# Decoding with an integer add, and TensorE turns for queries, keys and attention weights of two batches

## The chip, the cores and the metric

One core of a Trainium2 chip runs the whole program. The metric is device microseconds (us) from one launch to its end. A run of the kernel before stands at a median of 836.11 us over 3 runs.

## What is computed

Eight batches, eight heads, 576 tokens, head size 64, 32 memory slots.

```
a = softmax(phi, over the 32 slots)                # b h s m
k_m = einsum('bhsm,bhsd->bhmd', a, k)              # memory keys
v_m = einsum('bhsm,bhsd->bhmd', a, v)              # memory values
scores = (q @ k_m^T) / 8                           # b h s m
attn = softmax(scores, over the 32 slots)
x = (attn @ v_m), heads side by side               # 4608 x 512
h = x @ w_in;  g = relu(h)**2;  out = g @ w_out    # d_ff 2048
```

q, k, v and phi are float32. The two weights, w_in and w_out, are float64 and come to the device as pairs of 32-bit words (a low and a high word per number) and are decoded on the chip into a high and a low float32r part.

## The kernel before

**Planning.** Every operation is recorded by `op`, `vec` or `dma` with a guessed cost for each engine that may do it, with the buffers that it reads and writes, and with a due time. `Plan.order` then schedules them all: on each engine the ready operation with the earliest due time goes first; those marked `lead` are treated as due 9000 ns earlier. The result is one in-order list for each engine: TensorE (PE), VectorE (DVE), ScalarE (ACT), GpSimd (POOL) and SyncE (SP). SP issues nearly all loads, in its order. A buffer name (`tag`) has one or two slots; a new user of a slot waits until the last user is done.

**Work of a batch.** `memory` forms k_m and v_m for four heads (half `hh`), with phi, k and v in `phi` and `KV` tiles: a maximum on DVE (`mx`), two turns on PE (`pmx`), the exponential on ACT, then the sums and products `pkv` on PE (L421, L408). v_m goes into a block-diagonal tile `VT`, k_m into a turned block-diagonal tile `kb`. `attention` calls `scores` for each half: queries are turned in 32x32 blocks by DVE (`qT`, L527), multiplied on PE with `kb` as the stationary operand (`psc`, L532), turned back in 32x32 blocks by DVE into `S` (L536), normalised there (L544 to L551), turned a third time by DVE (`at`, L566) and split into two parts `ath` and `atl` (L260, L570).

**Weights and steps.** `decode` turns one 512 KB load of raw words (`raw`) into a weight tile; there are 16 pieces for w_in (`wi`) and 16 for w_out (`wo`), each a half of `piece`. `vw_alone` multiplies `VT` with a piece of w_in into `vw` (x @ w_in is formed as attn @ (v_m @ w_in)). `step` g does one tile of 128 of d_ff for one batch: `mm1` gives h (L603) and its squares `gh`, `glo`, `gl`; `mm2` adds them times `wo` into `acc` (L633, L634, L636).

**Decode** of one piece, on tiles of 128x512: the high word is clipped on DVE (L322), scaled on ACT (L323), its sign is taken (L324) and joined with the shifted rest (L325), giving the float `W`. Then the power of two of `W` is cut out (L326), the low word is multiplied by 2^-52 and by that power (L327), and the product is added to `W` (L330). ACT copies the sum into the high part; DVE subtracts (L339) to get the low part. For the pieces of w_out other than j = 0 (14 of 32) L330 is left out and the product is added to the low part by an accumulating DMA that POOL issues (L343).

**Order in the program.** Batch 0's memory and attention, then four times a piece of w_in, one of w_out and two steps of batch 0; batch 1's memory and attention and its first eight steps; then the other four pieces of each weight. From batch 2 on everything is decoded. Decoded w_in goes to DRAM too (L346) and is read back for later batches (L351). The tiles in which pieces are decoded (`raw` and `work`) are slots that other data uses later; the last pieces use the slots of `q` and `KV`.

Of the kernel before, what the change touches and what calls it, by code (L numbers as in the profile page):

```python
# [206 lines left out]
def tile_attention_moe(  # L207
# [97 lines left out]
    def decode(kind, j, h, room):  # L305
# [20 lines left out]
        vec({"DVE": ts(ND)}, lambda e: nc.vector.tensor_scalar(T(), W(), POWER, None, ALU.bitwise_and), [wk], [tk], lead=True)  # L326
        vec({"DVE": tt(ND)}, lambda e: nc.vector.scalar_tensor_tensor(tf(), low(), 2.0 ** -52, tf(), ALU.mult, ALU.mult), [rk, tk], [tk], lead=True)  # L327
        late = kind == "wo" and j > 0
        if not late:
            vec({"DVE": tt(ND)}, lambda e: nc.vector.tensor_add(wf(), wf(), tf()), [tk, wk], [wk], lead=True)  # L330
# [43 lines left out]
    def memory(b, hh, where=None):  # L374
# [70 lines left out]
        op({"PE": 300}, lambda e: nc.tensor.transpose(pv()[:, 0:P], vx().rearrange("p r d -> p (r d)"), ident), [vx], [pv], lead=True, lat=300)  # L445
        vh, vl = VT[b]
        for s in (0, 1):
            ch = 2 * hh + ((s + b) % 2)
# [4 lines left out]
            vec({"DVE": tt(64)}, lambda e, src=src, hi=hi, lo=lo: nc.vector.tensor_sub(lo(), src(), hi().bitcast(F32)),
                [pv, (vh, (ch, s))], [(vl, (ch, s))], port=None, lead=True)

# [218 lines left out]
    def evac(a, home, o, cols, add=False):  # L674
# [5 lines left out]
        for j in range(0, 4, n):  # L680
            b, c = cols[j]

            def store(d, j=j, b=b, c=c):
                rows = out[b * S:(b + 1) * S, :].rearrange("(p c) e -> c p e", c=NC)
                d(rows[c:c + n], o()[32 * j:32 * (j + n), :])
# [108 lines left out]
```

## Time and profile before

| | |
|---|---|
| three runs | 831.14, 836.11, 837.33 us |
| span of the profiled execution | 831.4 us, 12939 instructions |
| busy in the span | PE 763.5, DVE 571.2, ACT 378.1, POOL 67.4 us |
| mean granted TensorE clock | 0.973 |
| read from memory, written | 79.17 MB, 17.83 MB |

The page gives the profiled execution's span and no other time for it; the span stands beside the lowest of the three runs, 831.14 us. Rows of the page name a line, an engine, an operation, output<-input, and behind the bar the busy time in us, the mean duration of one in ns, and the idle time of the engine just before it with what ended it. PEld is the loading of stationary operands, which overlaps PE.

### The profile page before, as it was taken

The numbers are of one execution on the slowest core, as the hardware profiler recorded it, in microseconds if no ns is written. First come the engines' busy times: TensorE is split into PE (matmuls) and PEld (weight loads), VectorE is DVE, ScalarE is ACT, GpSimd is POOL, SyncE is SP. The second block draws the span as 40 slices with busy tenths as digits, with TensorE's granted clock in tenths as the row PEclk, the third lists the DMA queues.
The fourth block names the chain that finished last, engine by engine and source line by source line (L and its number), as shares of the span: only waits on it lengthen the run. The fifth ranks groups of instructions, "written<-read, shape, count | busy, mean of one in ns | idle before, by whom it ended". The sixth has DMA issues, their size and how long they took to land.

```text
span 831.4 us, 12939 instructions
## 1 busy us (share of the span) xinstructions
PE 763.5 (92%) x4756; PEld 643.3 (77%) x4756; DVE 571.2 (69%) x1266; ACT 378.1 (45%) x871; POOL 67.4 (8%) x105
## 2 busy tenths in 40 slices
PE   3468789989989899999999999999999999999995
PEld 2245578878768688888888888888788888888884
DVE  3899899898446756696768465786768556774540
ACT  1235466656535245563436355463435355552320
POOL 3113112222100100001000100000000100000000
PEclk9959999999999899999999999999999999999998
DMA  7947966657665443322552533323422433100001
GB/s 210 302 153 223 261 192 203 178 174 212 159 161 151 116 132 102 102 80 52 143 142 72 135 111 99 117 54 81 140 61 69 138 93 99 53 16 36 1 1 63
DMA packets 93091, 101.56 MB, mean 122 GB/s; under 512 B 24868, under 2 KB 78116, under 8 KB 93028
## 3 DMA queue, kind: packets, MB, share of 16 engines
q1 hardware_dynamic: 80292, 81.55, 33.2%
q0 software_dynamic: 12736, 19.19, 9.5%
q8 instruction: 37, 0.61, 0.3%
q14 instruction: 26, 0.21, 0.1%
HBM read 79.17 MB, written 17.83 MB: 117 GB/s over the span
## 4 chain that ended last, share of the span: by engine, by line
PE 73%; issue 10%; DVE 8%; DMA 3%; ACT 2%; POOL 2%; SPq 0%; POOLq 0%; DVEq 0%; ACTq 0%
PE h L603 20%; PE acc L636 12%; PE acc L633 12%; PE acc L634 12%; PE accl L659 4%; PE pvw L494 4%; PE psc L532 3%; PE pkv L408 3%; DMA q<-in_q_dram 2%; PE pvw L475 1%; DVE vw L503 1%; DVE qT L527 1%; ACT vw L260 1%; DMA wo<-work 1%; DVE work L325 1%
## 5 line engine op out<-in xcount | busy, mean ns | idle before, releaser
L603 PE MATMUL h<-ath,vw 128*128 128x320 f32 (+1 forms) x1024 | 213.9, 300 | 8.9 <-ACT ath L260 6.3
L633 PE MATMUL acc<-wo,gh 128*128 128x512 f32 x512 | 207.0, 404 | 2.7 <-ACT gh L609 2.5
L634 PE MATMUL acc<-wo,gh 128*128 128x512 f32 x512 | 201.7, 394 | 0.0
L603 PEld LDWEIGHTS h<-ath,vw 128*128 128x128 f32 x1024 | 172.5, 190 | 25.7 <-ACT ath L260 6.7
L636 PE MATMUL acc<-wo,glo 128*128 128x512 f32 x512 | 161.5, 409 | 3.0 <-DVE glo L613 2.8
L503 DVE TENSOR_TENSOR vw<-pvw,vw 64x256 fp32r<-64x256 f32 x192 | 78.5, 420 | 68.0 <-ACT vw L260 66.2
L633 PEld LDWEIGHTS acc<-wo,gh 128*128 128x128 f32 x512 | 97.1, 190 | 23.3 <-ACT gh L609 3.8
L260 ACT CAST vw<-pvw 64x256 fp32r<-64x256 f32 (+1 forms) x206 | 74.9, 381 | 83.9 <-PE pvw L494 37.6
L603 PE MATMUL h<-atl,vw 128*128 128x256 f32 (+1 forms) x512 | 110.5, 297 | 0.0
L634 PEld LDWEIGHTS acc<-wo,gh 128*128 128x128 f32 x512 | 96.9, 189 | 16.9
L636 PEld LDWEIGHTS acc<-wo,glo 128*128 128x128 f32 x512 | 90.5, 191 | 21.4 <-DVE glo L613 7.6
L609 ACT ACTIVATE gh<-r 128x512 fp32r<-128x512 f32 x128 | 80.7, 631 | 45.3 <-DVE r L608 38.5
L613 DVE TENSOR_TENSOR glo<-r,gh 128x512 fp32r<-128x512 f32 x128 | 87.6, 684 | 5.1 <-ACT r L611 2.9
L608 DVE TENSOR_SCALAR r<-h 128x256 f32<-128x256 f32 (+1 forms) x109 | 49.7, 458 | 59.0 <-PE h L603 58.1
L607 ACT ACTIVATE r<-h 128x256 f32<-128x256 f32 (+1 forms) x147 | 58.8, 407 | 67.8 <-PE h L603 59.8
L603 PEld LDWEIGHTS h<-atl,vw 128*128 128x128 f32 x512 | 83.0, 190 | 0.5 <-DVE atl L570 0.2
L611 ACT ACTIVATE r<-r 128x576 f32<-128x576 f32 x93 | 63.7, 685 | 2.1
L610 ACT ACTIVATE gl<-r 128x64 fp32r<-128x64 f32 x128 | 32.7, 256 | 63.2 <-DVE r L608 61.0
L659 PE MATMUL accl<-wo,gl 128*128 128x512 f32 x192 | 53.0, 400 | 0.1
L532 PE MATMUL psc<-qT,kb 128*128 128x256 f32 (+1 forms) x128 | 43.3, 465 | 5.8 <-DVE S L536 3.1
L494 PE MATMUL pvw<-wi,VTh 128*128 128x256 f32 x192 | 38.1, 290 | 3.8 <-DVE vw L503 3.7
L659 PEld LDWEIGHTS accl<-wo,gl 128*128 128x128 f32 x192 | 35.4, 191 | 7.3 <-DVE o L260 0.5
(94 smaller groups left out, 818.5 us busy)
## 6 DMA issues: line engine op xcount, KB each, us to landing
wi<-w_in_hi SPq DMA_DIRECT2D x56, 256.0 KB
wi<-w_in_lo SPq DMA_DIRECT2D x56, 256.0 KB
q<-in_q_dram SPq DMA_DIRECT2D x32, 288.0 KB
KV<-in_k_dram SPq DMA_DIRECT2D x32, 256.0 KB
KV<-in_v_dram SPq DMA_DIRECT2D x32, 256.0 KB
raw<-in_moe_w_in_dram SPq DMA_DIRECT2D x16, 512.0 KB
raw<-in_moe_w_out_dram SPq DMA_DIRECT2D x16, 512.0 KB
out_dram<-o POOLq DMA_DIRECT2D x20, 256.0 KB, 8.4
```

Of the source, the lines that this page charges most:

```text
L260: nc.scalar.copy(o, i) if e == "ACT" else ENG[e].tensor_copy(o, i)
L494: nc.tensor.matmul(pw()[:, x * SL:(x + 1) * SL], l()[:, 2 * hh + x, :], w(r, x), start=(i == 0), stop=(i == 2))
L503: vec({"DVE": tt(SL)}, lambda e, V=V, pr=pr, src=src: nc.vector.tensor_sub(V()[pr, 1, hh, :], src(), V()[pr, 0, hh, :].bitcast(F32)), [pw, ...
L532: nc.tensor.matmul(pq()[:, 0:32 * n], kb()[:, x].rearrange("p h m -> p (h m)"), qT()[:, x, 0:n].rearrange("p c t -> p (c t)"), start=(x == ...
L603: nc.tensor.matmul(p()[:, 0:n], V()[:, l, hh, c0:c0 + P], x()[:, hh, cs], start=(i == 0), stop=(i == 5))
L609: op({"ACT": act(SM)}, lambda e: nc.scalar.activation(gh(), r()[:, 0:SM], AF.Square), [r], [gh])
L611: op({"ACT": act(S), **({} if b < 2 else {"DVE": tt(S)})}, lambda e: nc.scalar.activation(r(), r(), AF.Square) if e == "ACT" else nc.vecto ...
L613: vec({"DVE": tt(SM)}, lambda e: nc.vector.tensor_sub(glo(), r()[:, 0:SM], gh().bitcast(F32)), [r, gh], [glo])
L633: nc.tensor.matmul(a(), gh()[:, c], t()[:, 0], start=f0, stop=False)
L634: nc.tensor.matmul(a(), gh()[:, c], t()[:, 1], start=False, stop=False)
L636: nc.tensor.matmul(a(), glo()[:, c], t()[:, 0], start=False, stop=f1)
L659: nc.tensor.matmul(a(), G()[:, l, :], t()[:, w], start=(ff == 0 and n == 0), stop=(ff == NFF - 1 and n == 2))
```

## The change

It has two parts.

*Decode.* The low word is converted by ACT in place, in the raw tile, with a scale of 2^-29, from uint32 to uint32, that is rounded to an integer in units of the last place of `W`. DVE then adds that integer to the bits of `W`. The cut of the power (L326), the product (L327) and the accumulating DMA (L343) go; all 32 pieces are added in the same way.

*Batches 0 and 1.* `memory_turned` and `attention_turned` take the place of the end of `memory` and of `attention`. Products with an identity on PE, which land in PSUM, turn k_m (together with v_m), the queries (`pq`, and `pql` for the 64 tokens left of 576) and the weights (`pat`, `patl`). Scores now have the queries as the stationary operand and `kb` as the moving one, so that they land with tokens on partitions (`psc`, `left`) and the normalising reads them from PSUM. Batch 0 uses the two PSUM slots `h`, batch 1 the one slot `pa`. Queries are loaded as 128x2x256 and 64x2x64 instead of as 64x1152, four DMAs for a half instead of two. Output rows of the two batches are stored in the order that follows from this.

```diff
-        vec(.. tensor_scalar(T(), W(), POWER, None, ALU.bitwise_and), [wk], [tk], lead=True)
-        vec(.. scalar_tensor_tensor(tf(), low(), 2.0 ** -52, tf(), ALU.mult, ALU.mult), [rk, tk], [tk], lead=True)
-        late = kind == "wo" and j > 0
-        if not late:
-            vec(.. tensor_add(wf(), wf(), tf()), [tk, wk], [wk], lead=True)
+        op({"ACT": act(ND)}, .. activation(low(), low(), AF.Copy, scale=2.0 ** -29), [rk], [rk], lead=True)
+        vec({"DVE": tt(ND)}, .. tensor_tensor(W(), W(), low(), ALU.add), [rk, wk], [wk], lead=True)
...
-        if late:
-            dma(.. d(out=part(1), in_=tf(), accum_op=ALU.add), 4096 * P, [tk, k1], [k1], eng="POOL", lead=True)
...
+        if b < 2:
+            memory_turned(b, hh, u, pk, rs, KV[0][0])
+            return
...
+    def memory_turned(b, hh, u, pk, rs, KV):
...
+        kb = kTs[b, hh] = st([P, 4, 2, M], F32, "kb", f"kb{u}", 2)
+        op({"POOL": 250}, lambda e: nc.gpsimd.memset(kb(), 0.0), [], [kb], lead=True)
+        vec({"DVE": 290}, .. tensor_scalar_mul(kd(), two(0), rs()), [pk, rs], [KV], ..)
+        vec({"DVE": 350}, .. vx() = two(1) * rs() * par ..)
+        for i, x, t in ((1, kd, KV), (0, vx, vx)):
+            op({"PE": 150}, .. nc.tensor.transpose(pv()[:, i * P:(i + 1) * P], x().., ident), ..)
+        for x in (0, 1):
+            op({"ACT": act(P), "DVE": tt(P)}, .. copy(e, kb()[pr, :, x, :], pv()[pr, P:2 * P]..), ..)
+        values(b, hh, pv)
...
+    def attention_turned(b):
...
+        bank = lambda name: pt("h", name, 2) if b == 0 else pt("pa", name)
+        late = pt("pv", f"left{b}")
...
+            for x in (0, 1):
+                pq = bank(f"pq{u}_{x}")     # four transposes of Q, 128x128, then a copy to qT
...
+            pq = bank(f"pql{u}")            # four transposes of QL, 64x64, then a copy to rest
...
+            psc = bank(f"psc{u}")
+            def mm(e, psc=psc, qT=qT, kb=kb):
+                for h in range(4):
+                    for y in (0, 1):
+                        nc.tensor.matmul(s4[:, 2 * y:2 * y + 2, h, :], qT()[:, h, y, :], kb()[:, h].., start=True, stop=True)
...
+            softmax(Sm, psc, NMAIN * P, psc, Sm, u)
+            if hh == 1:
+                softmax(Sl, lambda: late()[:, 0:P], P, late, (rest, 2), f"l{b}")
+        for hh in (0, 1):
+            pat = bank(f"pat{b}_{hh}")      # four transposes of Sm, a copy to ath, a difference to atl
...
+        pat = bank(f"patl{b}")              # one transpose of Sl, a copy to ath, a difference to atl
...
-    attention(0)
+    attention_turned(0)
...
-    attention(1)
+    attention_turned(1)
```

The planner gives a new order on every engine. Three places, before and after; lines of after.py differ from those of the kernel before.

The first instructions of PE, before: the turns for the first half of batch 0, then its sums with `ones` and its products with k and v.

```order
L393 MATMUL pmx_0_102<-ident,mx_0_95 128x128
L396 MATMUL pmx_0_102<-ident,mc_0_106 128x128
L421 MATMUL pkv_0_116<-ones,phi_0_78 32x1 x20
L408 MATMUL pkv_0_116<-KV_0_0_84,phi_0_78 32x128 x2
L408 MATMUL pkv_0_116<-KV_0_1_97,phi_0_78 32x128 x2
```

The same place in the changed kernel; `pq` are the turned queries, `q` their load.

```order
L386 MATMUL pmx_0_104<-ident,mx_0_95 128x128
L389 MATMUL pmx_0_104<-ident,mc_0_110 128x128
L521 MATMUL pq_0_0_171<-ident,q_0_117 128x128 x4
L521 MATMUL pq_0_1_183<-ident,q_0_117 128x128
L414 MATMUL pkv_0_121<-ones,phi_0_78 32x1 x20
L401 MATMUL pkv_0_121<-KV_0_0_84,phi_0_78 32x128 x2
```

Five turns of queries now stand ahead of the sums of the first half.

SP's loads behind the first KV tiles, before: phi of the second half, its k and v, the queries of the first half, the first raw words.

```order
L359 DMA phi_1_91<-in_phi_dram 128x4x128
L360 DMA phi_1_91<-in_phi_dram 64x4x32
L359 DMA KV_1_0_113<-in_k_dram 128x2x256
L360 DMA KV_1_0_113<-in_k_dram 64x2x64
L359 DMA KV_1_0_113<-in_v_dram 128x2x256
L360 DMA KV_1_0_113<-in_v_dram 64x2x64
L359 DMA KV_1_1_141<-in_k_dram 128x2x256
L360 DMA KV_1_1_141<-in_k_dram 64x2x64
L359 DMA KV_1_1_141<-in_v_dram 128x2x256
L360 DMA KV_1_1_141<-in_v_dram 64x2x64
L515 DMA q_0_166<-in_q_dram 64x1152 x2
L320 DMA raw<-in_moe_w_in_dram 128x2x512 x2
```

The same place in the changed kernel (behind these come the other two loads of k and v for `KV_1_1`, the queries of the second half, `q_1`, and only then the first raw words).

```order
L352 DMA phi_1_91<-in_phi_dram 128x4x128
L353 DMA phi_1_91<-in_phi_dram 64x4x32
L509 DMA q_0_117<-in_q_dram 128x2x256
L510 DMA ql_0_119<-in_q_dram 64x2x64
L509 DMA q_0_117<-in_q_dram 128x2x256
L510 DMA ql_0_119<-in_q_dram 64x2x64
L352 DMA KV_1_0_146<-in_k_dram 128x2x256
L353 DMA KV_1_0_146<-in_k_dram 64x2x64
L352 DMA KV_1_0_146<-in_v_dram 128x2x256
L353 DMA KV_1_0_146<-in_v_dram 64x2x64
L352 DMA KV_1_1_176<-in_k_dram 128x2x256
```

The queries of the first half moved ahead of k and v of the second half, and those of the second half moved ahead of the first raw words.

DVE behind the exponential of the first half, before: the first blocks of queries, then decode.

```order
L527 STREAM_TRANSPOSE qT_0_0_205<-q_0_166 128x2x256
L322 TENSOR_SCALAR work<-raw 128x512
L324 TENSOR_SCALAR work<-raw 128x512
L433 TENSOR_SCALAR rs_1_271<-pkv_1_210 128x1
L434 RECIPROCAL rs_1_271<-rs_1_271 128x1
L325 SCALAR_TENSOR_TENSOR work<-work 128x512
L322 TENSOR_SCALAR work<-raw 128x512
L326 TENSOR_SCALAR work<-work 128x512
L324 TENSOR_SCALAR work<-raw 128x512
L327 SCALAR_TENSOR_TENSOR work<-raw,work 128x512
```

The same place in the changed kernel; `S` holds the exponentials of the first half's scores, `rz` their sums.

```order
L496 TENSOR_REDUCE rz_0_271<-S_0_252 128x16
L259 COPY rest_205<-pql_1_266 64x256
L497 TENSOR_SCALAR rz_0_271<-rz_0_271 128x16
L498 RECIPROCAL rz_0_271<-rz_0_271 128x16
L499 TENSOR_TENSOR S_0_252<-S_0_252,rz_0_271 128x512
L321 TENSOR_SCALAR work<-raw 128x512
L323 TENSOR_SCALAR work<-raw 128x512
L426 TENSOR_SCALAR rs_1_364<-pkv_1_284 128x1
L324 SCALAR_TENSOR_TENSOR work<-work 128x512
L321 TENSOR_SCALAR work<-raw 128x512
L326 ISA work<-raw,work 128x1024
```

The end of the normalising of the first half (its maxima and differences stand just ahead of these rows) now comes before the first decode instruction, which used to come before any of it; the integer add is the instruction that reads 128x1024 elements.

More of the change, by code (lines that the diff above doesn't have):

```diff
@@ L340, in decode @@
             [wk, k0], [k1], lead=True)
-        if late:
-            dma(lambda d: d(out=part(1), in_=tf(), accum_op=ALU.add), 4096 * P, [tk, k1], [k1], eng="POOL", lead=True)
         if kind == "wi":
@@ L454, in memory @@
                 [pv, (vh, (ch, s))], [(vl, (ch, s))], port=None, lead=True)
+    def memory_turned(b, hh, u, pk, rs, KV):
+        vx = st([P, 2, D], F32, "vx", f"vx{u}")
+        kd = lambda: KV()[:, 0:2 * D].rearrange("p (r d) -> p r d", r=2)
+        two = lambda i: pk()[:, i * D:(i + 1) * D].rearrange("p (o d) -> p o d", o=1).broadcast_to([P, 2, D])
+        kb = kTs[b, hh] = st([P, 4, 2, M], F32, "kb", f"kb{u}", 2)
+        op({"POOL": 250}, lambda e: nc.gpsimd.memset(kb(), 0.0), [], [kb], lead=True)
+        vec({"DVE": 290}, lambda e: nc.vector.tensor_scalar_mul(kd(), two(0), rs()), [pk, rs], [KV], port=None, lead=True)
+        vec({"DVE": 350}, lambda e: nc.vector.scalar_tensor_tensor(
+            vx(), two(1), rs(), par.rearrange("p (r o) -> p r o", o=1).broadcast_to([P, 2, D]), ALU.mult, ALU.mult), [pk, rs], [vx], port=None, lead=True)
+        pv = pt("pa", f"pvt{u}")
+        for i, x, t in ((1, kd, KV), (0, vx, vx)):
+            op({"PE": 150}, lambda e, i=i, x=x: nc.tensor.transpose(pv()[:, i * P:(i + 1) * P], x().rearrange("p r d -> p (r d)"), ident),
+               [t], [(pv, i)], lead=True, lat=300)
+        for x in (0, 1):
+            pr = slice(64 * x, 64 * x + 64)
+            op({"ACT": act(P), "DVE": tt(P)}, lambda e, x=x, pr=pr: copy(e, kb()[pr, :, x, :], pv()[pr, P:2 * P].rearrange("p (h m) -> p h m", h=4)),
+               [(pv, 1), kb], [(kb, x)], lead=True)
+        values(b, hh, pv)
@@ L683, in store @@
             def store(d, j=j, b=b, c=c):
[L684 to L685 removed]
+                rows = out[b * S:(b + 1) * S, :]
+                if b >= 2:
+                    rows = rows.rearrange("(p c) e -> c p e", c=NC)[c:c + n]
+                elif c < 4 * NMAIN:
+                    rows = rows[0:SM].rearrange("(p c) e -> c p e", c=NMAIN)[c // 4]
+                else:
+                    rows = rows[SM:S]
+                d(rows, o()[32 * j:32 * (j + n), :])
             dma(store, 32 * n * DM * 4, [home], [], eng="SP" if b >= B - 2 else "POOL")
```

76 lines of the change are left out of this document (72 added, 4 removed).

## The prediction

> **What bounds the kernel now.** I read the page's busy times first, then a table by stretches of the span (time, then busy us and count for PE, PEld, DVE, ACT, POOL, then granted clock, DMA share and GB/s), then who PE waits for.
>
> ```profile
> PE 763.5 (92%) x4756; PEld 643.3 (77%) x4756; DVE 571.2 (69%) x1266; ACT 378.1 (45%) x871; POOL 67.4 (8%) x105
> ...
> 0.00:57.40 57.40, 25.99 (x277) 15.90 (x277) 40.29 (x90) 13.61 (x25) 10.98 (x21) 0.84 0.73 218
> 57.40:110.00 52.60, 39.88 (x252) 30.46 (x252) 48.54 (x108) 24.94 (x56) 14.23 (x19) 0.92 0.84 239
> 110.00:170.00 60.00, 55.27 (x324) 48.36 (x325) 54.91 (x120) 38.06 (x84) 10.36 (x13) 1.00 0.63 186
> 170.00:210.00 40.00, 39.97 (x240) 35.63 (x240) 33.88 (x66) 25.43 (x55) 9.52 (x12) 1.00 0.68 194
> 210.00:290.00 80.00, 72.11 (x495) 58.41 (x494) 48.15 (x108) 33.26 (x80) 6.29 (x12) 0.94 0.58 149
> 290.00:360.00 70.00, 69.85 (x396) 61.10 (x395) 45.66 (x103) 36.38 (x94) 1.34 (x2) 0.99 0.39 114
> ```
>
> PE is idle for 831.4 - 763.5 = 67.9 us. Of that 31.4 lie before 57.4 us, when the first steps begin, 12.7 between 57.4 and 110, 4.7 up to 170, 7.9 between 210 and 290, 0.2 up to 360. What is left, 11 us, is nearly all the tail. So from 290 us on the kernel is bound by PE, and the change, which touches nothing there, can only move that part as a whole. Up to 110 us PE waits and DVE is the busy one: 48.5 of 52.6 us in the second stretch. All decode and both changed batches lie before 290 us; **the question is how much of 56.7 us of idle PE goes, and how much PE work comes.**
>
> **Term 1, DVE up to the fourth `vw` of batch 0**, the L483 at 106.7 us in the first row here. Below it stand the groups of DVE up to 107 us that the change removes or shortens (count | busy us, mean ns | idle):
>
> ```profile
> 106.70 0.68 DVE L483 TENSOR_TENSOR vw<-pvw,vw 128x512 fp32r<-128x512 f32 x1
> ...
> L327 DVE SCALAR_TENSOR_TENSOR work<-raw,work 128x512 f32<-128x512 uint32 x15 | 10.2, 679 | 0.0
> L330 DVE TENSOR_TENSOR work<-work 128x512 f32<-128x512 f32 x10 | 6.8, 679 | 0.0
> L326 DVE TENSOR_SCALAR work<-work 128x512 uint32<-128x512 uint32 x15 | 6.2, 415 | 0.0
> L527 DVE STREAM_TRANSPOSE qT<-q 128x512 f32<-128x512 f32 (+1 forms) x8 | 6.2, 770 | 2.9 <-PE psc L532 1.4 <-DMA q<-in_q_dram 1.4
> L536 DVE STREAM_TRANSPOSE S<-psc 128x256 f32<-128x256 f32 (+1 forms) x7 | 3.2, 454 | 2.2 <-PE psc L532 2.2
> L544 DVE TENSOR_REDUCE red_None<-S 128x18 f32<-128x576 f32 x3 | 2.2, 733 | 0.0
> L566 DVE STREAM_TRANSPOSE at<-S 128x256 f32<-128x256 f32 (+1 forms) x4 | 1.9, 468 | 0.0
> L570 DVE TENSOR_TENSOR atl<-at,ath 128x256 fp32r<-128x256 f32 (+1 forms) x4 | 1.8, 452 | 0.1
> L520 DVE TENSOR_TENSOR kb<-kT,bd 128x256 f32<-128x256 f32 x4 | 1.6, 400 | 0.0
> L545 DVE TENSOR_TENSOR S<-S,red_None 128x576 f32<-128x576 f32 x2 | 1.5, 750 | 0.0
> L548 DVE TENSOR_REDUCE rz_None<-S 128x18 f32<-128x576 f32 x2 | 1.5, 748 | 0.0
> L551 DVE TENSOR_TENSOR S<-S,rz_None 128x576 f32<-128x576 f32 x2 | 1.5, 746 | 0.0
> ```
>
> *Decode.* L327, L330 and L326 make 10.2 + 6.8 + 6.2 = 23.2 us. In the new order 14 integer adds stand ahead of that same `vw`. No row shows one. The first row here and L551 above bound it; the other two price copies out of PSUM and conversions on ACT:
>
> ```profile
> L613 DVE TENSOR_TENSOR glo<-r,gh 128x512 fp32r<-128x512 f32 x128 | 87.6, 684 | 5.1 <-ACT r L611 2.9 <-PE acc L636 0.5
> L260 DVE COPY o<-acc 128x512 f32<-128x512 f32 x14 | 9.3, 688 | 4.2 <-PE acc L636 4.0
> L323 ACT ACTIVATE work<-work 128x512 f32<-128x512 f32 x32 | 20.1, 627 | 21.5 <-DVE work L322 21.5
> ```
>
> A two-tile instruction over 512 words takes 0.68 us, and 64 more elements (L551, 746 ns) cost 0.062 us, so 0.97 ns each. The add reads 128x1024 halves of 16 bits: 0.68 us if a word still costs one element, 0.68 + 512 x 0.97 ns = 1.18 us if a half does. I take 0.68, since bytes and shape of output are those of L330, and L327 reads the same strided raw words in 679 ns. 14 x 0.68 = 9.5, which saves 13.7 us; at 1.18 it would save 6.7. [...]
>
> *Attention.* The other nine groups make 21.4 us. In their place the new order has, up to the same `vw`, eleven instructions over 512 scores (0.68 each, as L330: 7.5), four over 128 scores and four products for k_m over 128 (0.68 - 384 x 0.97 ns = 0.31 each: 2.5), two differences for `atl` over 512 and one over 128 (1.7), one copy of queries out of PSUM (0.69), three copies over 256 and one over 128 (0.43 and 0.31: 1.6): 14.0. That saves 7.4. Reciprocals and other small instructions are about as many as before. One more maximum of phi (1.29, row below) and one more `glo` stand ahead too, and one L339 fewer: +1.3.
>
> Together 13.7 + 7.4 - 1.3 = 19.8 us of durations. Durations overlap:
>
> ```profile
> 44.77 0.68 DVE L325 SCALAR_TENSOR_TENSOR work<-work 128x512 uint32<-128x512 uint32 x1
> 45.38 0.42 DVE L322 TENSOR_SCALAR work<-raw 128x512 f32<-128x512 f32 x1
> 45.71 0.42 DVE L326 TENSOR_SCALAR work<-work 128x512 uint32<-128x512 uint32 x1
> ```
>
> Two instructions of 0.68 + 0.42 us take 0.94 from start to start, 0.86 of it. So **term 1 is -19.8 x 0.86 = -17 us** of DVE time (-11 if the add costs 1.18).
>
> **Term 2, the start.** PE's list now has five turns of queries ahead of `pkv`, so `pkv` waits for the queries' load, and they come behind phi of the second half:
>
> ```profile
> 7.93 0.61 SPq L360 DMA_DIRECT2D phi<-in_phi_dram  x1
> ...
> 11.23 1.29 DVE L391 TENSOR_REDUCE mx<-phi 128x128 f32<-128x640 f32 x1 [2.85 <-DMA phi<-in_phi_dram]
> ...
> 10.54 0.81 PE L421 MATMUL pkv<-ones,phi 128*32 128x1 f32 x40 [3.01 <-ACT phi L399]
> ...
> 21.10 0.43 DVE L322 TENSOR_SCALAR work<-raw 128x512 f32<-128x512 f32 x1 [0.34 <-DMA raw<-in_moe_w_in_dram]
> ```
>
> phi's last issue ended at 8.54 us and its reader began at 11.23, 2.7 us later. Issues follow each other by 0.64 us, so the four DMAs of the queries end at 11.1 and land at about 13.9. `pkv` then starts at 13.9 instead of 10.54: +3.4. Behind it hang, in a chain, k_m, scores, the normalising of the first half (four instructions of 0.68 on DVE, an exponential on ACT) and, behind that on DVE's list, the subtraction for the second half and all decode, which began at 21.1 before. With an estimate of 3 us each for `pkv`, for k_m's turn and copies, and for scores, and 4 for the rest, it begins at 27. DVE does other work meanwhile, but with less of it ready I add 1 for waits on PE in that chain: **+4 us**. Below, if the queries land with phi's, 0; above, all of the 6 us by which decode begins later.
>
> Terms 1 and 2 bring the fourth `vw` 13 us forward.
>
> **Term 3, what PE gives back.** A turn on PE is shown alone and matmuls in a row:
>
> ```profile
> L532 PE MATMUL psc<-qT,kb 128*128 128x256 f32 (+1 forms) x128 | 43.3, 465 | 5.8 <-DVE S L536 3.1
> ...
> L393 PE MATMUL pmx<-ident,mx 128*128 128x128 f32 x16 | 4.9, 308 | 8.3 <-DVE par L282 6.2 <-DVE VTl L453 1.5 <-DVE S L536 0.6
> ...
> 77.86 1.43 PE L408 MATMUL pkv<-KV,phi 128*32 128x128 f32 x40
> ...
> 100.71 0.72 PE L475 MATMUL pvw<-wi,VTh 128*128 128x256 f32 x4
> ```
>
> Before, a batch has 16 matmuls of L532, 43.3 / 8 = 5.4 us. The change has 35 turns (16 of queries, 8 of left-over queries, 9 of weights, 2 more of k_m) and 48 short matmuls of scores for it. A turn costs 0.18 (L475's pace, four in 0.72) to 0.31 us (L393 alone), a short matmul 0.036 (L408's pace, forty in 1.43) to 0.18 (L475's). That is 8 to 19.5 us, a net of +2.6 to +14 for a batch. Turns come four in a row, so I take L475's pace; scores have the full 128x128 stationary operand of L475 but a quarter of its columns, so the middle, 0.1: 6.3 + 4.8 = 11, a net of +5.7. Batch 0's part lies in the 31.4 us of idle PE. Batch 1's lies in the stretch up to 110 us, where PE has 12.7 idle. With DVE's 13 us gone, PE would have 39.9 + 5.7 = 45.6 us of work in about as much time. Neither engine then has slack to wait for the other, so I let **3 of the 13 us** go to their waits on each other: -10 up to there. ACT gets 32 conversions at 0.63 us (L323's row, 20 us in all) and copies; at 24.9 of 52.6 busy it has room, and if a raw load is late they hold the squares (L609) behind them on ACT, as L322 holds DVE today.
>
> **Term 4, later waits.** PE's waits from 57 to 360 us that matter, and the chain ahead of one:
>
> ```profile
> PE pvw L494 <- DVE vw L503: 3.4, 1, 3.4
> PE pkv L408 <- DMA KV<-in_v_dram: 3.0, 1, 3.0
> ...
> PE pvw L475 <- DVE vw L483: 2.5, 2, 2.2
> ...
> 160.58 5.14 DMA wo<-work
> ...
> SPq L359 <- DMA wo<-work: 7.6, 1, 7.6
> ```
>
> The wait of 2.2 us hangs on an accumulating DMA of 5.14 us that held a `work` tile, and SP waited 7.6 us for another before it could load k and v into the slot of the last pieces. These DMAs are gone. I take back the 2.2 and 1.8 of the other 6.4: **-4**. Next late there are loads that wait for `pkv` to free its two KV slots, which stay. Nothing at all comes back if those bind first, 10 if all of it goes.
>
> **Sum.** -10 - 4 = -14 us, on a span of 831.4: 817.4. The median of the runs stands 4.7 above the span, which I let stand: **822 us**.
>
> **Rivals.**
> - *Both engines interlock without waits and the later idle goes:* -13 and -10: 813 us. For it: PE has no idle from 170 to 210 although DVE is 85% busy. 0.17.
> - *The add costs 1.18 us.* 14 x 0.5 x 0.86 = 6 of the -10 is lost, and some of term 4: 829 us. Against it: the row of L330. 0.17.
> - *Loads bind instead.* DMA was at 0.84 of its engines between 57 and 110 us, and the same bytes are wanted earlier. Then only term 4 is left, or nothing, as if the change had not done what it says: 832 to 836. 0.14.
> - *Slower: one PSUM slot.* Batch 1's eleven new uses of `pa` (four and two for queries, two of scores, three of weights) each need PE to write and ACT or DVE to empty it, and PE's list is in order. PE's longest waits for DVE in a row above are 2.2 and 3.4 us; at 2.3 each, 25 us, it is +11: 847. At 1.3 us each the gain is gone. Against it: the planner puts steps of batch 0 between the uses. 0.08.
> - *Forecast:* 815 to 829. 0.44.
>
> A measurement of this kernel can tell about 1%, 8 us, from no change. Faster by more (under 828): 0.38 of the forecast, the first rival and a third of the second, 0.61. Slower by more: 0.07. The range leaves out the last rival and the lower half of the first: 810 to 838.
>
> **What would show it.** Fourth `vw` of batch 0 at about 95 to 98 us on DVE; the integer add at 0.68 us; first `pkv` near 13.9 us and first decode near 27; PE's idle time ahead of its closed stretch down from 56.7 to about 32, its busy time up by some 11 us; no wait on an accumulating DMA. It is wrong if the add stands above 0.9 us, if PE waits for copies out of `pa` by more than 1.3 us a time, or if the order of loads and not DVE ends the waits before 100 us.

## The result, and the profile after

The changed kernel takes **823.7 us** (median of 4 runs, 821.4 to 825.8) where the kernel before takes 834.6 beside it: a ratio of 0.987, with an interval of [0.983, 0.991]. That is 10.9 us less, against 822 forecast in a range of 810 to 838. The span of the profiled execution went from 831.4 to 823.8 us.

The page of the changed kernel, busy times:

```profile
PE 775.6 (94%) x4890; PEld 656.5 (80%) x4890; DVE 544.7 (66%) x1209; ACT 396.2 (48%) x908; POOL 54.3 (7%) x95
```

PE's busy time rose by 12.1 us (763.5 before), and its idle time in the span fell from 67.9 to 823.8 - 775.6 = 48.2 us. DVE lost 26.5 us, ACT gained 18.1. The table by stretches, with the columns of the one before (time, PE, PEld, DVE, ACT, POOL, granted clock, DMA share, GB/s):

```profile
0.00:57.40 57.40, 34.79 (x350) 26.03 (x350) 31.36 (x75) 18.37 (x35) 12.55 (x26) 1.00 0.67 201
57.40:110.00 52.60, 44.61 (x322) 36.97 (x323) 43.80 (x94) 35.34 (x75) 8.90 (x13) 0.89 0.74 240
110.00:170.00 60.00, 57.88 (x335) 51.36 (x333) 46.92 (x103) 43.26 (x94) 7.31 (x10) 0.95 0.54 176
170.00:210.00 40.00, 37.92 (x257) 32.72 (x256) 33.13 (x69) 22.48 (x49) 4.61 (x7) 1.00 0.66 192
210.00:290.00 80.00, 78.92 (x520) 64.67 (x519) 54.06 (x118) 37.39 (x92) 4.96 (x11) 1.00 0.49 143
```

PE's idle time up to 290 us is now 22.6 + 8.0 + 2.1 + 2.1 + 1.1 = 35.9 us, where it was 56.7. Between 57 and 110 us DVE is no longer the engine without room: it idles 8.8 us there (4.1 before), while ACT went from 24.9 to 35.3 us busy. The single rows that the prediction named, on PE and DVE (start, duration, what it is, and in brackets the wait ahead of it):

```profile
12.14 1.11 PE L521 MATMUL pq<-ident,q 128*128 128x128 f32 x4 [5.37 <-DMA q<-in_q_dram]
13.84 0.82 PE L414 MATMUL pkv<-ones,phi 128*32 128x1 f32 x40
29.20 0.42 DVE L321 TENSOR_SCALAR work<-raw 128x512 f32<-128x512 f32 x1
101.61 0.69 DVE L604 TENSOR_TENSOR vw<-pvw,vw 128x512 fp32r<-128x512 f32 x1 [0.19 <-ACT vw L259]
```

The first sums stand at 13.84 us (13.9 forecast), the first decode at 29.2 (27), the fourth `vw` of batch 0 at 101.6 (95 to 98; 106.7 before). The integer add, as DVE's group up to 107 us:

```profile
L326 DVE CUSTOM_DVE_ANT_0 work<-raw,work 128x1024 uint16<-128x1024 uint16 x15 | 10.2, 679 | 0.0
```

0.679 us, the lower bound and the value taken.

So the total came out, but the fourth `vw` came forward by 5 us and not by 13. Just ahead of it, at 98 us, PE has its longest wait between 57 and 290 us. The chain of work that ended last shows what it waits for:

```profile
90.70 0.51 DVE work L326
91.21 5.26 DMA raw<-in_moe_w_out_dram
96.47 0.02 issue
96.49 0.05 ACT raw L325
96.54 0.51 issue
97.05 0.61 ACT S L495
97.66 0.48 ACT qT L259
98.14 0.04 issue
98.18 0.33 PE pq L521
```

Read downwards: DVE's integer add frees a raw tile, the next raw load takes 5.26 us into it, ACT's conversion of its low words (L325, new) stands in ACT's order and waits for that load, an exponential and a copy of queries out of the single PSUM slot `pa` stand behind it, and PE waits for that copy before it can turn the next queries. The same place on ACT and on PE, each with its wait:

```profile
96.49 0.65 ACT L325 ACTIVATE raw<-raw 128x512 uint32<-128x512 uint32 x1 [4.00 <-DMA raw<-in_moe_w_out_dram]
```

```profile
98.18 0.33 PE L521 MATMUL pq<-ident,q 128*128 128x128 f32 x1 [2.74 <-ACT qT L259]
```

And right behind PE's wait its granted clock goes from 1.00 to 0.50, and it stays there from 98.8 to 116.0 us. This is PE's stretch from 98 to 116 us (busy, clock, DMA share, GB/s):

```profile
98.00:116.00 18.00, 15.55 (x73) 0.53 0.48 165
```

The matmuls into `acc` (L754, L755) start 0.23 us apart at 93 us, at a clock of 1.00, and 0.43 us apart at 115 us, at 0.50. So 15.55 us busy at 0.53 is, as an estimate, 8.2 us of work at full clock in 18 us. The text below calls the wait and the slow clock behind it the stall.

### The profile page after: what moved, and what is told of

Read it like the earlier page. It is cut to its first block, busy times and chain, and to the rows that moved or that the text cites. A ratio compares the mean times of both kernels' runs of the same rounds, so it can differ in the third digit from the quotient of the medians.

```text
span 823.8 us, 13149 instructions
## 1 busy us (share of the span) xinstructions
PE 775.6 (94%) x4890; PEld 656.5 (80%) x4890; DVE 544.7 (66%) x1209; ACT 396.2 (48%) x908; POOL 54.3 (7%) x95
## 4 chain that ended last, share of the span: by engine, by line
PE 76%; DVE 8%; DMA 6%; ACT 6%; issue 2%; SPq 1%; ACTq 0%; DVEq 0%
PE h L724 20%; PE acc L754 12%; PE acc L757 12%; PE acc L755 12%; PE accl L780 5%; PE pvw L615 4%; DMA raw<-in_moe_w_out_dram 3%; PE psc L653 3%; PE pkv L401 2%; DMA raw<-in_moe_w_in_dram 2%; PE pvw L596 1%; PE psc L541 1%; ACT vw L259 1%; DVE glo L734 1%; DVE work L326 1%
## 5 line engine op out<-in xcount | busy, mean ns | idle before, releaser
L724 PE MATMUL h<-ath,vw 128*128 128x320 f32 (+1 forms) x1024 | 211.1, 299 | 2.5 <-ACT r L728 2.2
L754 PE MATMUL acc<-wo,gh 128*128 128x512 f32 x512 | 206.5, 403 | 1.5 <-ACT gh L730 1.2
L755 PE MATMUL acc<-wo,gh 128*128 128x512 f32 x512 | 201.5, 394 | 0.0
L724 PEld LDWEIGHTS h<-ath,vw 128*128 128x128 f32 x1024 | 170.6, 190 | 18.0 <-ACT r L728 4.9
L754 PEld LDWEIGHTS acc<-wo,gh 128*128 128x128 f32 x512 | 96.8, 189 | 22.4 <-ACT gh L730 3.1
L724 PE MATMUL h<-atl,vw 128*128 128x320 f32 (+1 forms) x512 | 110.0, 296 | 0.0
L755 PEld LDWEIGHTS acc<-wo,gh 128*128 128x128 f32 x512 | 96.7, 189 | 16.6
L259 ACT CAST vw<-pvw 64x256 fp32r<-64x256 f32 (+1 forms) x199 | 71.0, 373 | 79.3 <-PE pvw L615 47.2
L757 PEld LDWEIGHTS acc<-wo,glo 128*128 128x128 f32 x512 | 90.0, 190 | 20.5 <-DVE glo L734 6.7
L729 DVE TENSOR_SCALAR r<-h 128x320 f32<-128x320 f32 (+1 forms) x110 | 50.2, 458 | 60.1 <-PE h L724 59.4
L732 ACT ACTIVATE r<-r 128x576 f32<-128x576 f32 x98 | 67.0, 684 | 2.1
L615 PEld LDWEIGHTS pvw<-wi,VTh 128*128 128x128 f32 x192 | 31.1, 189 | 6.2 <-issue 2.5
```

Source lines behind the costliest of these rows:

```text
L259: nc.scalar.copy(o, i) if e == "ACT" else ENG[e].tensor_copy(o, i)
L615: nc.tensor.matmul(pw()[:, x * SL:(x + 1) * SL], l()[:, 2 * hh + x, :], w(r, x), start=(i == 0), stop=(i == 2))
L724: nc.tensor.matmul(p()[:, 0:n], V()[:, l, hh, c0:c0 + P], x()[:, hh, cs], start=(i == 0), stop=(i == 5))
L732: op({"ACT": act(S), **({} if b < 2 else {"DVE": tt(S)})}, lambda e: nc.scalar.activation(r(), r(), AF.Square) if e == "ACT" else nc.vecto ...
L754: nc.tensor.matmul(a(), gh()[:, c], t()[:, 0], start=f0, stop=False)
L755: nc.tensor.matmul(a(), gh()[:, c], t()[:, 1], start=False, stop=False)
```

## The experiments

Two questions were open: which half of the change brings the 11 us, and whether the stall at 98 us is what keeps the rest away. All kernels in one table; the idle time is the span less PE's busy time, both from each profiled execution.

| kernel | median us | ratio to before, interval | span | PE busy | PE idle |
|---|---|---|---|---|---|
| before | 834.6 | | 831.4 | 763.5 | 67.9 |
| changed | 823.7 | 0.987 [0.983, 0.991] | 823.8 | 775.6 | 48.2 |
| decode_only | 824.7 | 0.985 [0.981, 0.989] | 824.5 | 759.8 | 64.7 |
| turns_only | 832.9 | 0.996 [0.992, 0.999] | 833.4 | 782.1 | 51.3 |
| no_accum | 832.9 | 0.996 [0.993, 0.999] | 829.1 | 763.6 | 65.5 |
| turn_b0 | 823.7 | 0.984 [0.980, 0.989] | 822.3 | 771.1 | 51.2 |
| raw4 | 826.9 | 0.990 [0.986, 0.993] | 825.6 | 776.1 | 49.5 |
| low_to_t | 815.1 | 0.976 [0.973, 0.979] | 814.3 | 771.6 | 42.7 |
| raw_slow | 816.2 | 0.977 [0.971, 0.982] | 817.2 | 772.6 | 44.6 |
| b1_h | 814.3 | 0.974 [0.970, 0.978] | 814.4 | 771.5 | 42.9 |
| ctl_pe | 824.0 | 0.986 [0.980, 0.992] | 822.3 | 774.0 | 48.3 |
| ctl_wire | 825.3 | 0.987 [0.981, 0.994] | 824.9 | 776.7 | 48.2 |
| decode_t | 817.4 | 0.979 [0.973, 0.985] | 812.9 | 755.7 | 57.2 |
| both | 814.5 | 0.975 [0.970, 0.981] | 813.1 | 765.1 | 48.0 |

The kernel before took 833.8 to 835.9 us beside the three sets of experiments.

Totals alone do not say where a kernel gains or loses. The next table does. The products into `h`, `acc`, `accl`, `pvw` and `pkv` are the same in every kernel. For each trace I counted how many columns of them are left at a given time, and took the time at which the changed kernel has as many left. The table has the difference: minus is ahead of the changed kernel, plus is behind it. At 130 us the attention of batches 0 and 1 is finished on PE in all of them. It is one profiled execution each, and the two controls differ from the changed kernel by up to 2.5 us.

| kernel | at 130 us | at 210 us | at 290 us |
|---|---|---|---|
| before | 0.0 | +1.6 | +11.8 |
| decode_only | -9.1 | -10.2 | +0.8 |
| turns_only | +6.0 | +8.3 | +9.7 |
| no_accum | +2.5 | +2.2 | +5.0 |
| turn_b0 | -2.8 | -4.4 | -0.2 |
| raw4 | +1.0 | +0.4 | +1.3 |
| low_to_t | -6.3 | -8.3 | -8.8 |
| raw_slow | -0.2 | -0.9 | -3.9 |
| b1_h | -3.6 | -7.1 | -9.1 |
| ctl_pe | -0.4 | -1.6 | -2.0 |
| ctl_wire | +0.8 | -2.5 | +0.5 |
| decode_t | -12.4 | -13.9 | -9.4 |
| both | -9.0 | -10.9 | -10.5 |

The changed kernel is level with the kernel before at 130 us and has gained 1.6 us at 210. It gains nearly all of its time between 210 and 290 us.

### The two halves apart

**decode_only**: the kernel before with the new decode, and the old attention.

```diff
-        vec({"DVE": ts(ND)}, lambda e: nc.vector.tensor_scalar(T(), W(), POWER, None, ALU.bitwise_and), [wk], [tk], lead=True)
-        vec({"DVE": tt(ND)}, lambda e: nc.vector.scalar_tensor_tensor(tf(), low(), 2.0 ** -52, tf(), ALU.mult, ALU.mult), [rk, tk], [tk], lead=True)
-        late = kind == "wo" and j > 0
-        if not late:
-            vec({"DVE": tt(ND)}, lambda e: nc.vector.tensor_add(wf(), wf(), tf()), [tk, wk], [wk], lead=True)
...
-        if late:
-            dma(lambda d: d(out=part(1), in_=tf(), accum_op=ALU.add), 4096 * P, [tk, k1], [k1], eng="POOL", lead=True)
...
+        op({"ACT": act(ND)}, lambda e: nc.scalar.activation(low(), low(), AF.Copy, scale=2.0 ** -29), [rk], [rk], lead=True)
+        vec({"DVE": tt(ND)}, lambda e: nc.vector.tensor_tensor(W(), W(), low(), ALU.add), [rk, wk], [wk], lead=True)
```

> The kernel before with the new decode alone (rounded low word as an integer, no accumulating DMA), attention as before. Theory A (the two halves of the change add: decode takes 13.7 us of durations off DVE ahead of the fourth vw and frees the tiles that the accumulating DMAs held; attention takes 7.4 us off DVE but gives PE 6 us a batch and starts 3 us later): decode has most of it, about 8 of the 11 us, 826 to 827 where the kernel before has 834.6. Rival B (DVE's decode is hidden, the turns have nearly all): 831 to 834. Rival C (either half alone clears DVE enough for the chain through PE and ACT to bind, so the halves do not add): 823 to 825.

**turns_only**: the changed kernel with these lines turned back, so that it has the turns and the old decode.

> The changed kernel with the old decode (cut, float product, float add, accumulating DMAs), queries, keys and weights of two batches still turned on TensorE. Theory A (halves add, turns have the smaller one): 3 us under the kernel before, about 831. Rival B (turns have nearly all): 824 to 826. Rival C (halves do not add, either gives all): 824 to 826 here and 823 to 825 with decode alone. Rival D (with old decode the start, later by 8 us at the first decode row, is not paid back): 836 to 842, slower than before.

Measured: 824.7 us for decode alone, 832.9 for the turns alone. Decode alone takes off as much as the whole change. The turns have 3 us on the old decode and nothing that can be told on the new one. Theory A had the order of the halves right and their sizes wrong. Rival C's range came for decode (823 to 825) and not for the turns (824 to 826). Apart, the halves bring 11.3 + 3.0 = 14.3 us, together 10.9, so they do not quite add. The pages of decode_only and of turns_only:

```profile
PE 759.8 (92%) x4756; PEld 641.1 (78%) x4756; DVE 554.3 (67%) x1224; ACT 393.2 (48%) x895; POOL 54.7 (7%) x91
```

```profile
PE 782.1 (94%) x4890; PEld 661.7 (79%) x4890; DVE 560.4 (67%) x1246; ACT 386.5 (46%) x889; POOL 67.5 (8%) x109
```

Where the turns are added, PE's idle time falls by 16.6 us (67.9 to 51.3) or 16.5 (64.7 to 48.2), and its busy time rises by 18.6 (763.5 to 782.1) or 15.8 (759.8 to 775.6). Between two kernels of about the same span these two must be nearly alike, so that this alone does not say that the turns only fill waits. Decode alone, in the stretches of PE (busy, clock, DMA share, GB/s):

```profile
57.40:110.00 52.60, 45.66 (x303) 0.89 0.72 224
110.00:170.00 60.00, 58.17 (x344) 1.00 0.54 173
210.00:290.00 80.00, 69.25 (x427) 0.91 0.51 127
```

PE is busy 5.8 and 2.9 us longer than before in the first two stretches, and 2.9 us less in the last. The table of leads shows what the equal totals hide. At 210 us decode_only is 11.8 us ahead of the kernel before and 10.2 ahead of the changed kernel. So the turns cost some 10 us up to there (6.7 on the old decode). Between 210 and 290 us decode_only then loses 11.0 us against the changed kernel. Nearly all of PE's idle time in this stretch is one wait, at 220.6 us, the longer of the two in this row of PE's waits up to 300 us (total, times, longest):

```profile
PE pvt L439 <- DVE vx L435: 12.0, 2, 10.7
```

DVE forms `vx` only behind the maximum of a phi that is being loaded for a later batch, and waits 11.37 us for that load. The load in decode_only, and the same place in the changed kernel, from the chains that ended last:

```profile
214.30 13.81 DMA phi<-in_phi_dram
...
222.91 4.79 DMA phi<-in_phi_dram
```

Beside that load run the four stores of 256 KB of batch 1's output rows. In decode_only, where batch 1 keeps its old order of output rows, they take a median of 12.4 us from issue to landing (DMA view from 205 to 232 us), in the changed kernel 4.2. The changed order of output rows, which the sections ahead of the prediction name in one sentence, is thus a likely source of what the turns give back. The two other kernels with the new decode and the old rows in batch 1 also wait for such a load: turn_b0 for 4.8 us at 231.7, for k and v, and decode_t for 5.1 us at 223.1, for phi. no_accum has the old rows too and no such wait over 2 us. No run changes the order of the rows alone, so that this cause is argued and not shown.

**no_accum**: the kernel before without accumulating DMAs.

```diff
-        late = kind == "wo" and j > 0
+        late = False
```

> The kernel before with its float add on DVE for every piece, so no accumulating DMA; 22 more adds of 0.68 us, 15 us of DVE, most of them after 60 us. It prices the hold of tiles by those DMAs apart from DVE's time. Theory A (their hold is what made the later waits of 2.2 and 3.4 us and SP's of 7.6 us, worth 4 to 7 us; DVE has room after 110 us but not before): those waits go, and the 15 us of adds cost about as much as they bring: 832 to 836. Rival (DVE's time is all that counts, holds are worth nothing): 15 x 0.86 x a half or more, 841 to 848. Rival (holds are worth it and DVE's time after 60 us is free): 827 to 830.

Measured: 832.9 us, ratio 0.996. The expectation miscounted: 14 pieces change, not 22, so 14 x 0.68 = 9.5 us of adds come (DVE's busy time rose by 7.4, from 571.2 to 578.6). The first theory's range held. The later waits that were named went or shrank: PE's busy time between 210 and 290 us is 77.29 us, where it was 72.11. Others of 2.5 and 2.0 us came, so that PE's idle time from 110 to 290 us fell from 12.6 to 9.0.

```profile
57.40:110.00 52.60, 41.01 (x257) 0.86 0.71 225
210.00:290.00 80.00, 77.29 (x501) 0.98 0.56 146
```

So the hold of tiles by these DMAs is worth a few us even where DVE has to pay for it. Of decode's 11 us some 3 or more are this. That the rest is DVE's time is likely, but no run shows it apart.

**turn_b0**: batch 1 back on the old attention.

```diff
-        if b < 2:
+        if b < 1:
             memory_turned(b, hh, u, pk, rs, KV[0][0])
...
-    attention_turned(1)
+    attention(1)
```

Batch 1's output rows go back to the old order with it.

> The changed kernel with batch 1 back on the old attention (blocks turned on DVE); batch 0 still turned on TensorE. Theory A (batch 1's turns take 3.7 us off DVE and give 6 us to PE in a stretch where PE has little room, so they are worth about nothing): within 3 us of the changed kernel, 821 to 827. Rival (the single PSUM slot of batch 1 costs): 815 to 820. Rival (both batches pay alike, through DVE): 827 to 830.

Measured: 823.7 us, the same as with both batches. PE's busy time is 4.5 us shorter and its idle time 3.0 longer. In total, turning batch 1 is worth nothing, as theory A had it. It is again a sum of two parts: turn_b0 is 4.4 us ahead at 210 us and loses that in its wait of 4.8 us at 231.7.

### The stall at 98 us

**raw4**, **low_to_t**, **raw_slow** and **b1_h** each aim at another link of the chain shown above: the shortage of raw tiles, ACT's wait for the load, ACT's place in the order, and the single PSUM slot. low_to_t does two things: ACT's conversion waits for DVE's shift in place of the load, and the raw tile is free after the conversion in place of DVE's add.

```diff
 raw4
-        0: ("V6 V7 W6a", "W6b W7a W7b V4 V5"), ...
+        0: ("V6 V7 W6a W6b", "W7a W7b V4 V5"), ...
 low_to_t
-        ... nc.scalar.activation(low(), low(), AF.Copy, scale=2.0 ** -29), [rk], [rk], lead=True)
-        ... nc.vector.tensor_tensor(W(), W(), low(), ALU.add), [rk, wk], [wk], lead=True)
+        ... nc.scalar.activation(T(), low(), AF.Copy, scale=2.0 ** -29), [rk], [tk], lead=True)
+        ... nc.vector.tensor_tensor(W(), W(), T(), ALU.add), [tk, wk], [wk], lead=True)
 raw_slow
-                o.end = wire + LANDS[e]
+                o.end = wire + LANDS[e] + o.slow     (2500 for loads of raw words, else 0)
 b1_h
-        bank = lambda name: pt("h", name, 2) if b == 0 else pt("pa", name)
+        bank = lambda name: pt("h", name, 2)
```

> The changed kernel with four tiles for raw words and four for work in place of three and five (W6b moved from the one list to the other), for the first sixteen pieces. In the changed kernel the chain runs from the integer add, which frees a raw tile, over the next raw load (5 to 6 us) to ACT's conversion of the low words, and what stands behind that on ACT in order (exponentials, copies of queries, squares) is what PE waits for; ACT stands 13.7 us ahead of such conversions between 40 and 290 us. Theory E (this wait is what eats the turns' gain): ACT's wait for raw loads falls under 6 us, the clock's dip near 100 us goes, 816 to 820. Rival F (DVE's busy time binds still, the late load is only the last of several equal ends): 822 to 826. Rival G (work tiles were the scarce ones): 826 to 832.

> The changed kernel with the rounded low word written into the work tile's first half, which is free behind the shift, and no longer in place. The raw tile is free after ACT's conversion, not after DVE's add, and ACT's conversion now waits for DVE's shift instead of for the load; the add's second operand is dense and no longer strided. Theory E (ACT's wait for raw loads is the bound): that wait is gone, the wait for the shift takes part of its place, 818 to 823. Rival H (the longer chain shift, conversion, add costs 1.3 us on each of the pieces on the path): 826 to 834. [...]

> The changed kernel with one number of the planner changed: a load of raw words is taken to land 2.5 us later than before (nearer to the 5 to 6 us that the trace shows), so that ACT's conversions are put later in ACT's order. Nothing else is added or taken away. Theory E: ACT's wait for raw loads falls from 13.7 to under 8 us and PE's waits on ACT with it, 817 to 821. Rival F (another order of the same work only moves the waits): 822 to 827.

> The changed kernel with batch 1's queries, scores and weights in the two PSUM slots of h, as batch 0's are, in place of the single slot pa. Theory E (PE's wait of 2.7 us at 98 us hangs on ACT standing before a raw load, not on the slot): same within 3 us of the changed kernel, 821 to 827, and PE still waits for a copy on ACT there. Rival R (the slot's turn-around is the cost, as in the prediction's slower rival): the wait and the low clock behind it go, 816 to 820.

Measured: 826.9, **815.1**, 816.2 and **814.3** us. Three of the four take 7.5 to 9.4 us off the changed kernel, all three more than any expectation had (818 to 823 for low_to_t, 817 to 821 for raw_slow, 816 to 820 for b1_h).

*low_to_t.* ACT's conversions before and after this edit, from ACT's groups between 20 and 290 us (busy, mean ns, idle ahead of them and its causes), the changed kernel first:

```profile
L325 ACT ACTIVATE raw<-raw 128x512 uint32<-128x512 uint32 x32 | 21.6, 676 | 13.8 <-DMA raw<-in_moe_w_out_dram 7.3 <-DMA raw<-in_moe_w_in_dram 6.4
```

```profile
L325 ACT ACTIVATE work<-raw 128x512 uint32<-128x512 uint32 x32 | 21.2, 670 | 5.9 <-DVE work L324 5.8
```

The wait for loads is gone, a shorter one for DVE's shift has come. PE's stretch and its scores there:

```profile
98.00:116.00 18.00, 18.00 (x124) 1.00 0.57 187
...
99.74 1.97 PE L541 MATMUL psc<-kb,qT 128*128 128x64 f32 x16
```

PE is busy all 18 us at full clock: 18.0 us of work against 8.2, and the median is 8.6 us lower. Rival H is out. Not all of these 10 us are gained: at 130 us low_to_t leads by 6.3, and it gains 2.5 more up to 290, where the changed kernel has no such stall.

*b1_h.* ACT still waits 12.2 us for raw loads ahead of its conversions (7.1 and 5.1), but PE does not wait for the copies behind them; its stretch is

```profile
98.00:116.00 18.00, 16.92 (x113) 1.00 0.25 84
```

The expectation had called this edit worth nothing under theory E. That was wrong, and rival R was right about the wait: the slot is a link of the same chain, and this stall is gone when either ACT's wait or the single slot is. But the edit does not price the stall. b1_h has a wait of 2.48 us of its own at 115 us, with 6.8 us at half clock behind it. At 130 us it leads by only 3.6 us, and the other 5.5 come between 130 and 290.

*raw4.* Theory E's forecast failed: ACT still waits 14.5 us for raw loads (8.2 and 6.3), and the time did not fall. A fourth raw tile does not shorten the wait. PE's wait of 2.74 us at 98 us is gone all the same. The stretch from 98 to 116 us has a clock of 0.72 though no wait of PE over 1.3 us stands there, and does 12.2 us of work at full clock against 8.2. Yet raw4 leaves it no earlier than the changed kernel (1.0 us behind at 130): it had fallen behind before, with a wait of 2.56 us at 75. So a milder stall alone brings no time, and why raw4 is not faster stays open.

*raw_slow.* Its time came out near the forecast (817 to 821 expected, 816.2 measured) but not by the forecast way: ACT's wait for raw loads is 12.6 us, not under 8. PE's wait at 98 us is gone; waits of 2.3 and 2.9 us stand at 87 and 110 us instead. The table of leads puts its gain late: 0.9 us at 210, 3.9 at 290. What brings its gain is not settled.

### Is it only another order?

Every edit changes the planner's list, so two controls change the list and nothing else.

```diff
 ctl_pe
-            op({"PE": 720}, lambda e, hh=hh: mm(e, hh), ...
+            op({"PE": 730}, lambda e, hh=hh: mm(e, hh), ...
 ctl_wire
-WIRE = 240.0
+WIRE = 242.0
```

> A control: the changed kernel with the planner's price of one group of products (the six matmuls of a vw half) at 730 in place of 720. No instruction is added, removed or resized; only the planner's list comes out in another order, from some 60 rows of PE on. Theory E (the three edits that gave 8 to 9 us did so by what they say): within 3 us of the changed kernel, 821 to 827. Rival N (the order is a lottery and the changed kernel drew a poor ticket, so any other order gains): 813 to 819.

> A second control: the changed kernel with the planner's rate of loads at 242 in place of 240; again only the order differs, from some 190 rows of PE on. Theory E: 821 to 827. Rival N: 813 to 819. If the two controls lie on both sides, the spread of orders is itself some 8 us and no single edit of that size is shown by its time alone.

Measured: 824.0 and 825.3 us, with the changed kernel's 823.7. Rival N, that any other order gains, is out. But both controls stay within 2.5 us of the changed kernel all the way, so that they try orders near its own. raw_slow, which also changes the order alone, gained 7.5 us. So an order can be worth as much as low_to_t and b1_h brought, and their times alone do not show their cause; what their traces show is that the stall is gone. Both controls keep the stall, at the same place; PE's row and its stretch, of ctl_pe and then of ctl_wire:

```profile
97.76 0.33 PE L521 MATMUL pq<-ident,q 128*128 128x128 f32 x1 [2.36 <-ACT qT L259]
...
98.00:116.00 18.00, 14.56 (x76) 0.62 0.47 167
```

```profile
97.84 0.48 PE L521 MATMUL pq<-ident,q 128*128 128x128 f32 x1 [3.09 <-ACT qT L259]
...
98.00:116.00 18.00, 15.74 (x73) 0.50 0.48 163
```

Estimated by the clock as above, 9.0 and 7.9 us of work in 18.

### The better decode without turns, and the two edits together

**decode_t** is decode_only with the edit of low_to_t; **both** is the changed kernel with low_to_t and b1_h.

> The decode-only kernel (attention as before) with the rounded low word written into the work tile, as in the version that took 815.1 with the turns. Theory E (ACT's wait for raw loads hid what the turns are worth; without turns DVE is the busy engine and ACT has less behind such a wait): within 4 us of decode alone, 821 to 826, and the turns are then worth 6 to 10 us. Rival I (the low word's place is worth 9 us to the decode by itself, the turns nothing): 814 to 818.

> The changed kernel with the low word written into the work tile and with batch 1 on the two slots of h: the two edits that took 815.1 and 814.3 alone. If they act in different places (the one on ACT's waits for loads, the other on PE's wait near 98 us and the low clock behind it): 806 to 811. If both remove the same stall or only pick another order: 812 to 817.

Measured: 817.4 us for decode_t, so writing the low word elsewhere is worth 7.3 us without any turn (its four runs, 814.9 to 821.0, lie below decode_only's 822.6 to 826.5). Rival I's range holds and theory E falls in its second half: ACT's wait did not hide what the turns are worth. The turns are worth 2.3 us on top (815.1 against 817.4, intervals overlapping). Where the edit pays is another place than with the turns: decode_t leads decode_only by 3.7 us at 210 and by 10.2 at 290, and in between its wait for phi is 5.1 us where decode_only's is 10.7. So the 7.3 us are not the price of the stall at 98 us. In decode_only there is no slot for turned queries to wait on, yet ACT stood longer still ahead of the conversions, from ACT's groups there:

```profile
L326 ACT ACTIVATE raw<-raw 128x512 uint32<-128x512 uint32 x32 | 21.7, 679 | 19.8 <-DMA raw<-in_moe_w_in_dram 10.0 <-DMA raw<-in_moe_w_out_dram 9.8
```

Both edits together take 814.5 us, no less than either. That is the range given for the same stall or for another order (812 to 817). At 130 us the two together are 9.0 us ahead, more than either alone, and at 290 they are 10.5 ahead, about 1.5 more than either. Its stretch:

```profile
98.00:116.00 18.00, 16.38 (x112) 1.00 0.23 68
```

## Why the prediction was right, point by point

The time was right in part by luck. The sum foretold a span of 817.4 us, and the profiled execution has 823.8. Added to it were 4.7 us by which the median stood above the span; in the changed kernel the median lies 0.1 us below it. As changes the two medians give -10.9 us where -14 was forecast. Nor do the places fit: -10 were to come up to the fourth `vw` and -4 later, but in the table of leads the changed kernel is level with the kernel before at 130 us, 1.6 ahead at 210 and 11.8 ahead at 290 (of which 7.6 are left in the spans). Of its signs of being right, PE's busy time (12.1 us more, some 11 forecast) and its idle time up to 290 us (35.9, about 32 forecast) nearly came. One of its signs of being wrong came too: PE waited 2.74 us for a copy out of `pa`, more than the 1.3 named.

- **Term 1, DVE.** The add's price held (0.68 taken, 0.679 measured). Its decode part, 13.7 x 0.86 = 11.8 us, is what decode alone shows: the fourth `vw` stands at 94.2 us in decode_only, 12.5 earlier than before, and its lead over the kernel before is 11.8 us at 210. Part of that may be the DMAs' hold of term 4. In the changed kernel the fourth `vw` came forward by only 5, so the turns took back 7.4. ACT's waits for loads are not the main reason: without them, in low_to_t, it stands at 99.8, and with them but with two slots, in b1_h, at 90.8. In b1_h decode also begins 15 us earlier (next point), so the slot alone is not shown to be the reason.
- **Term 2, the start.** The row came (13.84), and decode began 2 us later than said: the sixteen scores ahead of it took 3.67 us and not 16 x 0.1. But the +4 itself is not to be seen in the time. In b1_h and both the first decode begins at 14.58 and 14.87 us, in low_to_t at 29.27, and all three take 814 to 815 us. The row of b1_h:

```profile
14.58 0.43 DVE L321 TENSOR_SCALAR work<-raw 128x512 f32<-128x512 f32 x1 [1.84 <-DMA raw<-in_moe_w_in_dram]
```

  So when decode begins does not seem to bind in these three, which differ in other things too. No run moved the load of queries alone.
- **Term 3, PE's give-back.** Mis-sized twice. The work: the PE groups of the changed kernel up to 290 us (busy, mean ns, idle) are

```profile
L541 PE MATMUL psc<-kb,qT 128*128 128x64 f32 x64 | 13.0, 384 | 0.5 <-ACT rest L259 0.5
L521 PE MATMUL pq<-ident,q 128*128 128x128 f32 x32 | 7.7, 371 | 8.3 <-DMA q<-in_q_dram 5.6 <-ACT qT L259 2.7
```

  A 64-column score matmul averages 13.0 / 64 = 0.20 us where 0.1 was taken, a turn of queries 0.24 where 0.18 was. At the quicker pace of the row at 89.48 us below, a score matmul takes 1.90 / 16 = 0.12, so much of the excess is the slow pace at the start (3.67 us for sixteen, two times) and in the stall (3.74). PE's busy time rose by 16 us for two batches against decode_only, 8 a batch and not 5.7 (the bounds of 2.6 and 14 held). And the 3 us for the engines' waits on each other were too few. The prediction set 45.6 us of PE work against "about as much time", but 52.6 less the 13 is 39.6. Where the stall is gone, the kernels lead at 130 us by 3.6 (b1_h), 6.3 (low_to_t) and 9.0 (both). So an estimate of its cost is 4 to 9 us, with the other order of these kernels in it. The prediction had named the mechanism, a late raw load with work behind it on ACT, and had given it no price.
- **Term 4, later waits.** PE's idle time between 110 and 290 us went from 12.6 to 5.3 us, 7.3 less instead of 4. The accumulating DMAs are a part of it: without them alone, in no_accum, it is 9.0. But decode_only has none of them either and has 13.0, 10.7 of it the wait for phi. The prediction has no term for the order of output rows, which may be the rest.
- **The sum** held because these misses roughly cancel: the turns cost the changed kernel what decode had won up to 210 us, and the later waits gave far more than 4. The prediction had one sum for the whole change; apart, decode takes off as much as the whole, and the turns lose early about what they win late.
- **The rivals.** The add at 1.18 us is out by its row. Loads that bind were half right: they bind through ACT's order, at one place. The single slot `pa`, the slower rival, had the right place and the wrong count: not eleven waits of 2.3 us but one of 2.74, with 17.1 us at a clock of 0.50 behind it. The interlock without waits, at 813 us, is about what b1_h (814.3) and low_to_t (815.1) reach.

## What to carry to other kernels

When an operation is moved to an engine with an in-order list and made to read a freshly loaded tile, ask what stands behind it there: let it wait for something computed later, or give what stands behind it a second buffer. Run the halves of a change apart before believing that both pay, and ask of each where in the span it is ahead: here equal totals hid ten us lost early and about as many won late, where the order of output rows had changed too. Price a short wait of TensorE with the slow clock behind it (here 2.74 us of wait with 17.1 us at 0.50 behind it), and control for a planner's order with edits that change only the order, more than two and larger ones.

## What the runs showed of the hardware

- **A wait of 2.4 to 3.1 us came with 14 to 20.5 us at a granted clock of 0.50**, with PE 81 to 87% busy (14.56 to 15.74 of 18 us, mean clock 0.50 to 0.62), in three kernels with that wait; in three kernels without it (low_to_t, b1_h, both) the clock in that stretch was 1.00. The time at 0.50 is 17.1 us in the changed kernel; in ctl_pe it is two times 6.8 us, the second behind another wait of 1.84 us; in ctl_wire it is 20.5 us and begins inside the wait. In decode_only a wait of 2.6 us for a DMA (`wi`) at the same place was followed by 3.4 us only. That the wait causes the dip is argued from these kernels, and what sets its length is not shown; raw4 has a partial dip (0.72) without a wait over 1.3 us, and raw_slow one (0.81) beside its wait of 2.9 us at 110.
- **The same matmuls ran at two paces while the granted clock read 1.00.** In the changed kernel the clock is 1.00 both from 20.5 to 24.2 us and from 89.4 to 91.4; sixteen matmuls of the same form took 3.67 us in the first and 1.90 in the second. What made the first slower is not shown.

```profile
20.51 3.67 PE L541 MATMUL psc<-kb,qT 128*128 128x64 f32 x16
...
89.48 1.90 PE L541 MATMUL psc<-kb,qT 128*128 128x64 f32 x16
```

- **The integer add took the same time with a dense second operand**: in low_to_t, DVE's group is

```profile
L326 DVE CUSTOM_DVE_ANT_0 work<-work 128x1024 uint16<-128x1024 uint16 x32 | 21.7, 685 | 3.0 <-ACT work L325 2.6
```

  685 ns against 679 in the changed kernel with every second word skipped (the 15 adds up to 107 us; 683 over all 32): the stride of two words cost nothing here.
